# A one-row load moved to the head of the load queue of a fused decode kernel

## The chip, the cores and the metric

One core of a Trainium2 chip. The metric is the device time of one execution in microseconds (us). Most executions agree within a few tenths of a us. All runs here are of the fast state. Ratios are the mean time of one kernel's fast runs over the mean of the other's fast runs of the same rounds; they are not quite the ratio of the medians that are also quoted. The profiled span is about 1.3 us shorter than the device time (194.8 against 196.06 us in the profiled run of the kernel before).

## The reference

```python
W = min(4096, max(256, Sk // 4))                  # 4096 of 16384 cached positions
q = (x @ wq).reshape(B, Sq, Hq, Dh)               # B 4, Sq 1, Hq 32, Dh 128, D 512
k, v = k_cache[:, :, Sk - W:, :], v_cache[:, :, Sk - W:, :]     # 8 kv heads, each for 4 query heads
a = softmax(q @ k.T * Dh ** -0.5) @ v  ->  reshape @ wo
b = ((x @ W_gate) * (x @ W_gate > 0) * (x @ W_up)) @ W_down     # F 1792
g = sigmoid((x * gate_w).sum(-1, keepdims=True))
return g * a + (1 - g) * b
```

(Condensed; not literal code.) Inputs are bf16. The caches and weights that must be read come to 81 MB. `x` is 4 rows of 1 KB, and `gate_w`, the load that the change moves, is one row of 1 KB.

## The kernel before: the parts that matter

All loads are issued by the sync engine on one queue, in the order that `_dma_order` gives. The big ones go to four slots in turn; a load waits until its slot's last reader is done.

```python
def _dma_order():
    o = [("wq",), ("x",), ("gw",), ("k", 0), ("k", 1), ("v", 0)]
    for s in range(2, NSET):
        o += [("k", s), ("v", s - 1)]
    return o + [("wg",), ("wu",), ("v", NSET - 1), ("wd",)] + [("wo", p) for p in range(len(WO_PIECES))]
# ... in sync():
            if k == "x":
                load(("X",), "d_x", xsb[0:4, :], A_x.rearrange("b o d -> (b o) d"))
            elif k == "gw":
                load(("GW",), "d_gw", xsb[4:5, :], gate_w.rearrange("(o p) -> o p", o=1))
            elif k == "wq":
                load(("WQ",), "d_wq", slot("wq"), A_wq.rearrange("(p t) f -> p (t f)", t=4), waits=w)
# ... in tensor(): x and the gate row are transposed together, as five rows
        def XT():
            bk = bankb[tr(("XT",))]
            for q in range(4):
                tp(bk[:, 6 * q:6 * q + 5], xsb[0:5, q:q + 509:4], identb[0:5, 0:5], ev=("XT",) if q == 3 else None,
                   waits=tr_free(("XT",)) + [("X",), ("GW",), ("IDB",)])
# ... order of the program (cut): what TensorE does first and last
    o = [("CONST", k) for k in ("mask", "grp", "rfold")] + [("XT",), ("Z",), ("Q",), ("QT",), ("KT", 0, 0), ...
    o += [("SC", s, 3), ("SW", s), ("PV", s - 1), ("PT", s), ("RS", 1), ("GU",), ("PV", s), ("FFN",), ("OQ",)]
    return o + [("WO", p) for p in range(len(WO_PIECES))]
```

`PV` is the context product of one set of heads and needs its values; `OQ` folds the context; `WO` is the output product, whose weights are the last loads.

## Time and profile before

| | kernel before |
|---|---|
| median device time | 196.1 us (3 runs before the prediction, 196.01 to 196.16) |
| loads | 81.01 MB, mean 416 GB/s over the span |
| DVE busy / PE busy | 64% / 62% |

The sync engine's timeline of the kernel before: start us, duration us, what was issued.

```profile
0.80 0.40 SPq L256 DMA_DIRECT2D slots<-in_A_wq_dram  x1
1.26 0.35 SPq L256 DMA_DIRECT2D xsb<-in_A_x_dram  x1
1.66 0.22 SPq L256 DMA_DIRECT2D xsb<-in_gate_w_dram  x1
1.92 1.26 SPq L256 DMA_DIRECT2D slots<-in_A_k_cache_dram  x2
...
49.21 0.54 SPq L256 DMA_DIRECT2D slots<-in_A_k_cache_dram  x1
```

These durations are those of the issue, not of the transfer. The transfers are in the trace's packet records: the first 32 KB packet of the query weights starts at 1.81 us.

The timeline of TensorE at the end of the kernel before (in brackets the idle time before the group and what ended it):

```profile
178.49 5.03 PE L320 MATMUL bank<-slots,pT 128*64 128x512 bf16 x32 [5.70 <-DMA slots<-in_A_v_cache_dram]
183.45 1.69 PE L320 MATMUL bank<-slots,hg 128*4 128x256 bf16 x28
185.07 1.93 PE L320 MATMUL bank<-osb,fold 128*64 128x256 bf16 x16
188.07 2.02 PE L320 MATMUL bank<-slots,oq 128*4 128x256 bf16 x34 [1.06 <-DMA slots<-in_A_wo_dram]
190.83 1.15 PE L320 MATMUL bank<-slots,oq 128*4 128x256 bf16 x18 [0.73 <-DMA slots<-in_A_wo_dram]
192.20 0.82 PE L320 MATMUL bank<-slots,oq 128*4 128x256 bf16 x12 [0.23 <-DMA slots<-in_A_wo_dram]
```

TensorE waits for output weights three times: the loads set the end, and TensorE keeps up.

### The profile page before, as it was taken

The numbers are of one execution on the slowest core, as the hardware profiler recorded it, in microseconds if no ns is written. First come the engines' busy times: TensorE is split into PE (matmuls) and PEld (weight loads), VectorE is DVE, ScalarE is ACT, GpSimd is POOL, SyncE is SP. The second block draws the span as 40 slices with busy tenths as digits, with TensorE's granted clock in tenths as the row PEclk, the third lists the DMA queues.
The fourth block names the chain that finished last, engine by engine and source line by source line (L and its number), as shares of the span: only waits on it lengthen the run. The fifth ranks groups of instructions, "written<-read, shape, count | busy, mean of one in ns | idle before, by whom it ended". The sixth has DMA issues, their size and how long they took to land.

```text
span 194.8 us, 1734 instructions
## 1 busy us (share of the span) xinstructions
PE 120.6 (62%) x723; PEld 50.6 (26%) x723; DVE 124.1 (64%) x153; ACT 27.5 (14%) x34; POOL 9.5 (5%) x25
## 2 busy tenths in 40 slices
PE   0209279474943894686468943894586466743974
PEld 0003123121411341242112411341142122311562
DVE  6103769999399809980998199819981998370010
ACT  2213000040130013001300130013001300420100
POOL 7830000000000000000000000000000000000000
PEclk9999958999999797899876999697999889997899
DMA  6999999999999999999999999999999999999992
GB/s 215 431 432 431 437 437 431 431 427 451 431 437 437 446 427 424 431 437 431 431 431 431 427 424 437 444 437 431 431 431 421 431 395 427 470 431 384 425 404 90
DMA packets 3616, 81.10 MB, mean 416 GB/s; under 512 B 401, under 2 KB 666, under 8 KB 794
## 3 DMA queue, kind: packets, MB, share of 16 engines
q1 hardware_dynamic: 3610, 81.01, 97.3%
q8 instruction: 5, 0.08, 0.2%
q14 instruction: 1, 0.01, 0.0%
HBM read 81.01 MB, written 0.00 MB: 416 GB/s over the span
## 4 chain that ended last, share of the span: by engine, by line
DMA 54%; DVE 31%; PE 9%; issue 4%; SPq 0%; ACT 0%
DMA slots<-in_A_k_cache_dram 38%; DVE kt L491 21%; DMA slots<-in_A_wo_dram 10%; PE bank L320 7%; DMA xsb<-in_A_x_dram 6%; DVE sc L527 5%; DVE qblk L517 1%; PE bank L324 1%; DVE pT L542 1%; DVE rd L531 1%; SPq L256 0%; DVE negmax L537 0%; ACT gwB L600 0%; DVE osum L577 0%; DVE mx L527 0%
## 5 line engine op out<-in xcount | busy, mean ns | idle before, releaser
L491 DVE STREAM_TRANSPOSE kt<-slots 128x2048 f32<-128x2048 f32 x32 | 73.7, 2305 | 28.1 <-DMA slots<-in_A_k_cache_dram 28.0
L320 PE MATMUL bank<-kt,qblk 128*128 128x512 bf16 x256 | 72.1, 434 | 27.9 <-DVE kt L491 27.9
L320 PEld LDWEIGHTS bank<-kt,qblk 128*128 128x128 bf16 x256 | 25.2, 107 | 69.7 <-DVE kt L491 36.0
L320 PE MATMUL bank<-slots,pT 128*64 128x512 bf16 x256 | 32.3, 410 | 5.7 <-DMA slots<-in_A_v_cache_dram 5.7
L619 ACT ACTIVATE pe<-sc,negmax 128x2048 bf16<-128x2048 bf16 x8 | 16.0, 2002 | 60.1 <-DVE negmax L537 60.1
L527 DVE CUSTOM_DVE_ANT_0 sc<-bank,maskf 128x512 bf16<-128x512 f32 x32 | 21.0, 658 | 3.8 <-PE bank L320 3.7
L320 PEld LDWEIGHTS bank<-slots,pT 128*64 128x64 bf16 x256 | 15.1, 118 | 23.2 <-issue 13.4
L542 DVE STREAM_TRANSPOSE pT<-pe 128x2048 bf16<-128x2048 bf16 x8 | 18.5, 2312 | 2.2 <-ACT pe L619 2.2
L604 ACT ACTIVATE osb<-bank 128x512 bf16<-128x512 f32 x8 | 4.8, 597 | 81.5 <-PE bank L320 81.5
L320 PE MATMUL bank<-rd,grpb 128*128 128x32 bf16 x8 | 1.6, 194 | 22.1 <-DVE rd L531 22.1
L555 DVE TENSOR_TENSOR oq<-bank,recip 64x128 bf16<-64x128 f32 x2 | 0.9, 434 | 12.3 <-PE bank L320 12.2
L320 PEld LDWEIGHTS bank<-rd,grpb 128*128 128x128 bf16 x8 | 0.8, 98 | 25.7 <-DVE rd L531 25.7
L495 DVE COPY xT<-bank 128x20 bf16<-128x20 bf16 x1 | 0.2, 171 | 8.0 <-PE bank L324 8.0
L320 PE MATMUL bank<-slots,oq 128*4 128x256 bf16 x64 | 4.0, 272 | 2.0 <-DMA slots<-in_A_wo_dram 2.0
L320 PE MATMUL bank<-slots,xT 128*4 128x512 bf16 (+1 forms) x64 | 5.0, 467 | 0.0
L320 PE MATMUL bank<-maskr,maskl 128*128 128x512 bf16 x1 | 0.6, 609 | 5.9 <-POOL maskr L296 5.9
L517 DVE TENSOR_SCALAR qblk<-bank 32x64 uint32<-32x64 uint32 x16 | 2.9, 215 | 2.1 <-PE bank L324 2.1
L324 PE MATMUL bank<-identb,xsb 5*128 5x5 bf16 x4 | 0.3, 168 | 5.7 <-DMA xsb<-in_A_x_dram 5.7
L577 DVE CAST osum<-bank 4x256 bf16<-4x256 f32 x1 | 0.4, 418 | 5.2 <-PE bank L320 5.2
L320 PEld LDWEIGHTS bank<-slots,oq 128*4 128x4 bf16 x64 | 2.5, 84 | 3.5 <-DMA slots<-in_A_wo_dram 2.9
L296 POOL TENSOR_SCALAR_AFFINE_SELECT fold<-fold 128x256 bf16<-128x256 bf16 x8 | 3.3, 417 | 1.1
L486 DVE MEMSET qblk<- 128x2304 uint32 x1 | 2.0, 1978 | 1.3 <-PEq L644 1.3
(59 smaller groups left out, 40.3 us busy)
## 6 DMA issues: line engine op xcount, KB each, us to landing
slots<-in_A_k_cache_dram SPq DMA_DIRECT2D x8, 4096.0 KB, 25.1
slots<-in_A_v_cache_dram SPq DMA_DIRECT2D x8, 4096.0 KB, 30.5
slots<-in_A_wq_dram SPq DMA_DIRECT2D x1, 4096.0 KB, 12.4
slots<-in_A_wo_dram SPq DMA_DIRECT2D x1, 2176.0 KB, 17.1
slots<-in_B_W_gate_dram SPq DMA_DIRECT2D x1, 1792.0 KB, 19.7
slots<-in_B_W_up_dram SPq DMA_DIRECT2D x1, 1792.0 KB, 23.6
slots<-in_B_W_down_dram SPq DMA_DIRECT2D x1, 1792.0 KB, 18.5
slots<-in_A_wo_dram SPq DMA_DIRECT2D x1, 1152.0 KB, 19.5
```

Source lines behind the costliest of these rows:

```text
L296: op(lambda: e.affine_select(dst, src, pattern, cmp, fill, base=base, channel_multiplier=mult), ev)
L320: E.op(lambda: t.matmul(out_, lhsT, rhs, start=start, stop=stop, tile_position=pos, skip_group_check=True), ev=ev, waits=waits)
L324: E.op(lambda: t.transpose(out_, in_, idn), ev=ev, waits=waits)
L486: E.op(lambda: v.memset(qblk[:, :, :, :, :].rearrange("p s h c e -> p (s h c e)"), 0.0), ev=("QZ",))
L491: E.op(lambda: v.transpose(kt[:, f, :].bitcast(FP32), slot("k", s)[:, 4096 * f:4096 * f + 4096].bitcast(FP32)), ev=("E", "KT", s, f), waits=w)
L517: E.op(lambda dst=dst, r=r, g=g: v.tensor_scalar(dst, src[r, g, 0:B, :, :], 0, None, op0=ALU.bitwise_or), ev=("E",) + keys[1] if (q, g) == ...
L527: E.op(lambda: v.tensor_tensor_reduce(sc[:, 512 * f:512 * f + 512], banks[scb(key)], R["maskf"][:, :], 1.0, -3.0e38, ALU.add, ALU.max, mx4 ...
L531: E.op(lambda: v.tensor_tensor(rd32[:, :, :], bc(R["own8"][:, :].unsqueeze(2), 2, 4), bc(mx4[:, :].unsqueeze(1), 1, 8), ALU.mult), ev=("MA ...
L542: E.op(lambda: v.transpose(pT[:, s % 2, :], pe[:, :]), ev=("E", "PT", s), waits=[("EXP", s)] + ([("PV", s - 2)] if s >= 2 else []))
L555: E.op(lambda g=g, r=r: v.tensor_tensor(oq[r, :, :].rearrange("p i b -> p b i"), banks[tr(key)][0:64, 128 * g:128 * g + 128].rearrange("p ...
L604: E.op(lambda: a.activation(osb[:, s, :], ob(s), ACTF.Copy), ev=("NORM", s), waits=[("PV", s)])
L619: E.op(lambda: a.activation(pe[:, :], sc[:, :], ACTF.Exp, bias=negmax[:, s % 2:s % 2 + 1], scale=SCALE, accum_out=rowsum[:, s:s + 1]), ev= ...
```

## The change

The gate row's load is issued first of all, the query weights second and x third. The intent is to have the small load out of the way before the large ones fill the queue.

```diff
 def _dma_order():
-    o = [("wq",), ("x",), ("gw",), ("k", 0), ("k", 1), ("v", 0)]
+    o = [("gw",), ("wq",), ("x",), ("k", 0), ("k", 1), ("v", 0)]
```

Nothing else differs.

## The prediction

> What bounds the kernel now: one stream of loads. The DMA part of the profile shows 81.01 MB at a mean of 416 GB/s over the 194.8 us span; in the 40 slices DMA is busy 9 tenths or more in all but the first (6, 215 GB/s) and the last (2, 90 GB/s), at about 431 GB/s. No compute engine comes near: DVE is busy 64%, PE 62%. The packet records show 16 engines each moving a 32 KB row in 1.21 us, back to back from 2 to about 192 us. The issues on the sync engine show that the queue never runs dry: a key load lands 25.1 us after its issue in the median and takes 9.7 us of the stream. So time = start of the stream + bytes / rate + a tail (last landing 192.6; the last 12 matmuls, a cast of 0.42, the store, about 1.2 us).
>
> The chain of waits names other things (38% key loads, 31% DVE, 6% load of x), because it follows one consumer; its early part has slack behind the stream.
>
> What the change does. It removes, adds and resizes nothing. Before, the sync engine issues the query weights (4 MB) at 0.80, x (4 rows) at 1.26, the gate row (1 KB) at 1.66 and the first keys at 1.92 us. The gate row costs 0.27 us from start to start (0.22 busy). After: query weights near 1.06, x near 1.53, first keys still near 1.92.
>
> Gain: nearly none. The transposes of x and the gate row wait for both loads, and x still stands behind the 4 MB. The Trainium skill (DMA: Bandwidth & Descriptors, section Queues, rings and completion order) says each engine consumes its ring in order; the trace agrees: x lands at 13.14 and the gate row at 13.05, both with the last of the query weights (13.15). The same page (section Why a DMA increments its semaphore by 16 and not by 1) says that a one-row load runs on one engine; the gate row's semaphore has two updates only, which fits. Its packet leaves the stream of one engine (tens of ns) and lands near 3 us, of no use before x.
>
> Cost: the stream begins later by the gate row's issue, 0.27 us, all on the critical path, if the first packet still follows the issue of the query weights by 1.0 us (0.80 to 1.81 before). It may be less: the first packets are slow (1.9 to 2.3 us instead of 1.21), and if the gate row takes over part of a cold start, the shift shrinks towards 0. The front of compute (13.1 to 23 us) shifts as much, off the path.
>
> Predicted: 196.3 us, 195.9 to 196.7 eight times in ten. Chances: faster by over 2% 0.01, within 2% 0.98, slower 0.01.
>
> What would show it. Query weights issued near 1.06 us. First 32 KB packet at 2.0 to 2.1 us instead of 1.81. Gate row landing near 3 us; the x transposes still start at 13.2 to 13.5, released by x. The last landing of the output weights moves from 192.6 by as much as the first packet; the tail is unchanged, and so are the slices.
>
> What would make it wrong. A cold start that the tiny load absorbs: the time stays or falls by 0.1 to 0.3. A one-row first load that holds up issue for longer. A different balance between the 16 engines, whose last landings spread over some 2 us, so that another ends last.

## More of the kernel before

The page of the kernel before, three parts. The strings have one digit for each of 40 slices of the span; a 9 means 90% busy or more, PEclk is TensorE's granted clock in tenths.

```profile
span 194.8 us, 1734 instructions
PE 120.6 (62%) x723; PEld 50.6 (26%) x723; DVE 124.1 (64%) x153; ACT 27.5 (14%) x34; POOL 9.5 (5%) x25
...
PEclk9999958999999797899876999697999889997899
DMA  6999999999999999999999999999999999999992
GB/s 215 431 432 431 437 437 431 431 427 451 431 437 437 446 427 424 431 437 431 431 431 431 427 424 437 444 437 431 431 431 421 431 395 427 470 431 384 425 404 90
...
q8 instruction: 5, 0.08, 0.2%
```

The loads hardly pause between the first slice and the last. So the time is the moment at which this stream starts, plus its length, plus what remains after the last landing.

## The result

| | before | after |
|---|---|---|
| median, first comparison (6 runs each) | 196.08 us (195.98 to 196.16) | 196.5 us (196.4 to 196.82) |
| ratio | | 1.0026, 95% interval 1.0013 to 1.0038 |
| issue of the query weights, start to end | 0.80 to 1.20 | 1.18 to 1.54 |
| first 32 KB packet | 1.81 | 2.15 |
| gate row landed | 13.05 | 2.06 |
| x landed | 13.14 | 13.25 |
| last landing of output weights | 192.60 | 192.87 |
| issue of the store of the result | 193.54 | 193.93 |

The lower rows are of one profiled run of each kernel; packets are from the packet records, landings from the semaphore updates of the trace. The change costs about a quarter of a per cent.

The same parts of the page of the kernel after:

```profile
span 195.2 us, 1734 instructions
PE 122.2 (63%) x723; PEld 51.6 (26%) x723; DVE 124.3 (64%) x153; ACT 27.5 (14%) x34; POOL 9.5 (5%) x25
...
PEclk9999958999799699999789987699969799996699
DMA  6999999999999999999999999999999999998992
GB/s 215 430 431 430 430 430 430 430 426 443 430 430 430 445 436 433 430 436 430 436 430 430 433 436 443 430 436 430 430 436 426 423 387 426 477 430 382 430 398 78
```

The stream is as dense as before, within the digits. The sync engine's timeline after:

```profile
0.80 0.32 SPq L256 DMA_DIRECT2D xsb<-in_gate_w_dram  x1
1.18 0.37 SPq L256 DMA_DIRECT2D slots<-in_A_wq_dram  x1
1.59 0.32 SPq L256 DMA_DIRECT2D xsb<-in_A_x_dram  x1
1.95 1.25 SPq L256 DMA_DIRECT2D slots<-in_A_k_cache_dram  x2
```

The query weights start 0.38 us later, which is more than the 0.27 us that the gate row's place took when it stood third. The first keys are issued at nearly the same moment as before (1.95 instead of 1.92). Since the keys have to queue behind the query weights anyway, that does not help.

The end of TensorE's timeline after:

```profile
178.86 6.34 PE L320 MATMUL bank<-slots,pT 128*64 128x512 bf16 x32 [5.75 <-DMA slots<-in_A_v_cache_dram]
185.13 1.69 PE L320 MATMUL bank<-slots,hg 128*4 128x256 bf16 x28
186.76 1.94 PE L320 MATMUL bank<-osb,fold 128*64 128x256 bf16 x16
189.76 3.66 PE L320 MATMUL bank<-slots,oq 128*4 128x256 bf16 x64 [1.07 <-DVE oq L555]
```

In this execution the last context product took 6.34 us instead of 5.03. A stretch at half the TensorE clock, 6.8 us long, began at 177.5 us (the two sixes near the end of PEclk; the exact times are in the trace's clock records); in the profile before it was 3.4 us long from 177.9 us. All 64 output matmuls then ran without a wait, so here TensorE ended last. From the last landing to the store's issue took 1.06 us (193.93 − 192.87) instead of 0.94 (193.54 − 192.60). The chain of waits (the profile's path back from the last instruction, at each step to what released it) shows the same: before, it ended in the output weights' landing; after, it goes through TensorE.

```profile
171.74 20.41 DMA slots<-in_A_wo_dram
192.16 0.04 issue
192.20 0.87 PE bank L320 x12
```

That was the chain before; this is the chain after:

```profile
178.86 9.85 PE bank L320 x76
...
189.76 3.70 PE bank L320 x64
```

Is this second difference part of the change, or luck of one execution? That, and where the rest comes from, is what the experiments are for.

### The profile page after: what moved, and what is told of

It reads as the page before. It is cut to its first block, busy times and chain, and to the rows that moved or that the text cites. A ratio compares the mean times of both kernels' runs of the same rounds, so it can differ in the third digit from the quotient of the medians.

```text
span 195.2 us, 1734 instructions
## 1 busy us (share of the span) xinstructions
PE 122.2 (63%) x723; PEld 51.6 (26%) x723; DVE 124.3 (64%) x153; ACT 27.5 (14%) x34; POOL 9.5 (5%) x25
## 4 chain that ended last, share of the span: by engine, by line
DMA 40%; DVE 25%; PE 22%; issue 9%; POOL 2%; ACT 1%; POOLq 0%
DMA slots<-in_A_k_cache_dram 25%; PE bank L320 20%; DVE kt L491 18%; DMA slots<-in_A_v_cache_dram 15%; DVE sc L527 4%; PE bank L324 2%; DVE qblk L517 1%; POOL maskr L296 1%; DVE oq L555 0%; DVE rd L531 0%; DVE negmax L537 0%; ACT gwB L600 0%; ACT maskf L597 0%; POOL maskl L296 0%; POOL e L296 0%
## 5 line engine op out<-in xcount | busy, mean ns | idle before, releaser
L320 PE MATMUL bank<-slots,pT 128*64 128x512 bf16 x256 | 33.0, 416 | 5.8 <-DMA slots<-in_A_v_cache_dram 5.8
```

The source lines that it names most:

```text
L320: E.op(lambda: t.matmul(out_, lhsT, rhs, start=start, stop=stop, tile_position=pos, skip_group_check=True), ev=ev, waits=waits)
```

## The experiments

The theories:

- **A**: the whole stream starts later, because the gate row's issue holds the sync engine before the query weights. The cost is that issue and nothing else.
- **B**: the loss is in the tail, through half clock on TensorE there (**B2**: the end is the later of the loads and TensorE's last work, which makes the slow runs).
- **C**: a cold start of the DMA engines delays the first packets, and a small load ahead takes part of it over.
- **F**: run-to-run luck of which DMA engine has to fetch instructions.

All kernels gave correct results. Each run is compared with runs of the kernel before from the same rounds on the same chip: the first group stood on chip 0; e_gw_late and the three e_v7 on chip 6; e_gw_half and the three e_oq on chip 12. The edits are cut to the lines that matter. They are shown against the kernel before, except e_gw5 (against the changed kernel) and e_oq (against e_v7).

### First group: what stands ahead of the query weights

The kernel before in these rounds: median 196.15 us (195.92 to 196.39, 9 runs).

**e_after**: the changed kernel again, unedited.

> The changed kernel again, as the anchor of this group. Theory A (the stream of loads starts later because the gate row's issue stands ahead of the query weights): 196.4 to 196.6 us, ratio 1.0015 to 1.003; query weights issued near 1.18 us, first 32 KB packet near 2.15 us. Rival B (the loss sits in the tail: TensorE at half clock while the last context product runs) says the excess over the kernel before changes from run to run, with some runs near 196.1 and some near 196.8.

Measured: 196.53 us (196.19 to 196.81), ratio 1.0019 (1.0007 to 1.0032). Query weights issued at 1.17 us, first 32 KB packet at 2.14. In this profile TensorE waited for output weights again, so the loads ended last although there was a 6.8 us stretch of half clock from 175.7 us:

```profile
178.81 5.48 PE L320 MATMUL bank<-slots,pT 128*64 128x512 bf16 x32 [5.66 <-DMA slots<-in_A_v_cache_dram]
...
192.55 0.82 PE L320 MATMUL bank<-slots,oq 128*4 128x256 bf16 x12 [0.23 <-DMA slots<-in_A_wo_dram]
```

The profiled time was 196.42 us, as slow as the other profile (196.45). So the changed kernel is slower without the tail effect too. As B expected, the runs spread; but the kernel before spread by 0.47 us as well.

**e_gw5**: four more copies of the one-row load, into an unused tile, ahead of the gate row.

```diff
-    o = [("gw",), ("wq",), ("x",), ...
+    o = [("j", 0), ("j", 1), ("j", 2), ("j", 3), ("gw",), ("wq",), ("x",), ...
+                load(("J", it[1]), f"d_j{it[1]}", R["junk"][it[1]:it[1] + 1, :], gate_w.rearrange("(o p) -> o p", o=1))
```

> Four more one-row loads of the gate row into an unused tile stand ahead of everything; five small issues precede the query weights. A: each costs its issue, 0.27 to 0.38 us start to start, so the query weights are issued near 2.3 us instead of 0.80 and the time is before + 1.2 to 1.5, 197.3 to 197.6 us. Rival C (a fixed cold start of the DMA engines is what delays the first packets, and small loads ahead take it over): the first 32 KB packet comes less than 1.0 us after the query weights' issue, and the time is 0.3 to 0.5 us less than A says, below 197.2 us. B: no more than the changed kernel, 196.5 us.

Measured: 197.66 us (197.4 to 197.84), ratio 1.008 (1.0066 to 1.0093), just above A's band. The timeline of the sync engine:

```profile
0.80 1.18 SPq L257 DMA_DIRECT2D junk<-in_gate_w_dram  x4
2.02 0.25 SPq L257 DMA_DIRECT2D xsb<-in_gate_w_dram  x1
2.31 0.37 SPq L257 DMA_DIRECT2D slots<-in_A_wq_dram  x1
```

The first 32 KB packet came at 3.30 us, 0.61 us after the end of that issue, exactly as before the change (1.20 to 1.81). C falls: small loads ahead shorten nothing. B, which allowed 196.5 us, falls as the cause of this loss too.

**e_gw_x_first**: gate row, x, then the query weights.

```diff
-    o = [("wq",), ("x",), ("gw",), ...
+    o = [("gw",), ("x",), ("wq",), ...
```

> Gate row, then x, then the query weights. A: two issues ahead, query weights near 1.55 us, time before + 0.6 to 0.75, 196.7 to 196.9 us. x lands near 3 us and the transposes of x start near 6 us instead of 13.3; the query matmuls then start with the landing of the query weights near 13.5, some 1 us earlier than in the changed kernel, and that gains nothing. A theory that the front of compute is on the path expects a gain of up to 1 us against that.

Measured: 196.86 us (196.61 to 197.13), ratio 1.0037 (1.0024 to 1.0049), as A said; query weights issued at 1.47 us. x had landed at 2.51 us, its transposes ran at 7.39, and the query product waited for its weights alone:

```profile
13.77 3.58 PE L320 MATMUL bank<-slots,xT 128*4 128x512 bf16 x32 [4.84 <-DMA slots<-in_A_wq_dram]
```

That product started 1 us earlier than in the changed kernel (14.80). The kernel became slower all the same: an earlier front bought nothing, a later stream cost its delay.

**e_gw_act**: the gate row first of all, but from the scalar engine's queue.

```diff
-    o = [("wq",), ("x",), ("gw",), ...
+    o = [("wq",), ("x",), ...                 # sync engine
+        E.op(lambda: a.dma_start(xsb[4:5, :], gate_w.rearrange("(o p) -> o p", o=1)), ev=("GW",), ctr="d_gw")   # scalar engine, first
```

> The gate row is still issued first of all, but by the scalar engine's queue; the sync engine starts with the query weights at 0.80 us as in the kernel before, then x. A: the stream starts at 1.81 us again, and the time is that of the kernel before, 195.9 to 196.2 us, ratio 0.999 to 1.0005. If what costs is a gate-row packet or its early landing (not the issue slot on the sync engine), it stays at 196.4 to 196.6.

Measured: 196.23 us (195.91 to 196.48), ratio 1.0004 (0.9991 to 1.0016). The gate row is issued at 0.79 us and does not hold the sync engine:

```profile
0.79 0.50 ACTq L587 DMA_DIRECT2D xsb<-in_gate_w_dram  x1
0.79 0.40 SPq L256 DMA_DIRECT2D slots<-in_A_wq_dram  x1
```

The first 32 KB packet is at 1.81 us again, and the loss is not to be seen. So the early gate row itself costs nothing; its place on the sync engine does. The interval would still allow a small loss.

Put together, the delay of the end of the query weights' issue against the measured change (ratio − 1, times the 196.15 us of before):

| kernel | end of issue | delay | first 32 KB packet | change in time |
|---|---|---|---|---|
| before | 1.20 | 0 | 1.81 | 0 |
| e_gw_act | 1.19 | −0.01 | 1.81 | +0.08 |
| e_after | 1.51 | 0.32 | 2.14 | +0.37 |
| e_gw_x_first | 1.83 | 0.64 | 2.46 | +0.73 |
| e_gw5 | 2.68 | 1.48 | 3.30 | +1.57 |

The time follows the delay one to one, within 0.1 us, where each interval is about 0.25 us wide to either side.

The semaphore records show the same for the stream alone, without what comes after it. A big load lands in 16 parts, each with a semaphore update. I take the mean of the 16 for the last piece of the output weights that has 16, in the profile of each kernel. In the seven profiles of all groups (e_gw_late aside) whose first 32 KB packet comes at 1.81 to 1.84 us, this mean is 191.31 to 191.46, on average 191.40 us. In the four with the changed front it is 191.69 to 191.77, on average 191.72; in e_gw_x_first 191.99, in e_gw5 192.85. So the stream ends 0.32, 0.59 and 1.44 us later for delays of 0.32 to 0.35, 0.64 and 1.48 us.

### How much delay the front of compute can bear

**e_gw_late**: the gate row behind the first keys.

```diff
-    o = [("wq",), ("x",), ("gw",), ("k", 0), ("k", 1), ("v", 0)]
+    o = [("wq",), ("x",), ("k", 0), ("gw",), ("k", 1), ("v", 0)]
```

> Query weights, x, first keys, and only then the gate row. The transposes of x wait for a gate row that stands behind another 4 MB, so they start near 22.9 us instead of 13.2 and the whole front of compute is 9.7 us late. Theory A (only the start of the stream and its length count; the front has slack): 195.9 to 196.4 us, ratio 0.999 to 1.001. A theory that the front of compute sets the time (the chain of waits of the kernel before gave 6% to the load of x) expects up to 9.7 us more.

Measured: 197.05 us (196.73 to 197.9), ratio 1.0055 (1.0038 to 1.0071), against 196.13 us (11 runs of the kernel before in this group). A miss: I had taken the slack of the front to be larger than it is. The page and the timelines tell why. The transposes of x started at 23.03 us, and everything behind moved with them, including the release of the slots:

```profile
GB/s 221 435 436 435 442 455 441 435 435 441 425 428 328 428 428 423 428 431 428 428 428 428 428 428 425 428 428 428 435 448 415 438 412 427 458 441 395 436 394 83
```

```profile
23.03 0.27 PE L324 MATMUL bank<-identb,xsb 5*128 5x5 bf16 x4 [15.51 <-DMA xsb<-in_gate_w_dram]
...
59.87 0.54 SPq L256 DMA_DIRECT2D slots<-in_A_k_cache_dram  x1
```

One slice, near 60 us, fell to 328 GB/s. A key load that the kernel before issues at 49.21 us was issued at 59.87, and adding its issue (0.54) and the 0.61 us from issue to first packet, it could not move data before 61.0 us, while the packet records show the queue running out from 60.5 us. The loads lost about 1 us once and the kernel never got it back (the mean of the last output weights' landings is 192.49 us, 1.04 later than in the kernel before). So a front that is 9.8 us late is already too late.

**e_gw_half**: a delay half as long. The first keys are loaded in two halves with the gate row between them.

```diff
-    o = [("wq",), ("x",), ("gw",), ("k", 0), ("k", 1), ("v", 0)]
+    o = [("wq",), ("x",), ("ka",), ("gw",), ("k", 0), ("k", 1), ("v", 0)]   # ka: columns 0 to 8191 of the first keys
# (cut: ka is loaded into the first keys' slot, ("k", 0) loads the other half, and the reader waits for both)
```

> As e_gw_late, which lost 0.9 us because its front came 9.8 us late and a key load was issued at 59.9 us when the queue had just run dry (in the kernel before: 49.2 us). Here the first keys are loaded in two halves and the gate row stands between them, so the front is about 4.9 us late. A (the front has some 10 us of slack and a delay below it costs nothing): the key load that came at 59.9 comes near 54 to 55 us, DMA stays busy, 195.9 to 196.3 us, ratio 0.999 to 1.001. If a late front costs in proportion, about 0.45 us more than before.

Measured: 196.2 us (196.02 to 196.61), ratio 0.9999 (0.9986 to 1.0012), against 196.3 us for the kernel before (11 runs, 195.88 to 196.6). The transposes started 5.0 us later than before and the key load was issued 5.35 us later (54.56 instead of 49.21):

```profile
18.25 0.27 PE L329 MATMUL bank<-identb,xsb 5*128 5x5 bf16 x4 [10.72 <-DMA xsb<-in_gate_w_dram]
...
54.56 0.54 SPq L256 DMA_DIRECT2D slots<-in_A_k_cache_dram  x1
```

No loss is to be seen. A front that is 5 us late costs nothing measurable, so the few tenths by which the change moves it should not matter. The limit lies between 5 and 9.8 us; where exactly is not measured.

### The tail, and a version that might beat both

**e_v7**, **e_v7_gw**, **e_v7_act**: the last values are loaded ahead of the gate and up weights, with the front of before, of after, and with gate row and x issued by the scalar engine.

```diff
-    return o + [("wg",), ("wu",), ("v", NSET - 1), ("wd",)] + ...
+    return o + [("v", NSET - 1), ("wg",), ("wu",), ("wd",)] + ...
-    ... ("PT", s), ("RS", 1), ("GU",), ("PV", s), ("FFN",), ("OQ",)]
+    ... ("PT", s), ("RS", 1), ("PV", s), ("GU",), ("FFN",), ("OQ",)]
```

> The front of the kernel before; at the end the last values are loaded before the gate and up weights, and TensorE does their product before the gate and up product. The last context product is then over by about 180 us, so a half-clock stretch of TensorE there can no longer hold up the end. Theory B2 (the end is the later of two: the stream's last landing, or the last context product and what follows, which loses about 1.7 us for 3.4 us more at half clock): the fast runs of the kernel before stay (195.9 to 196.1), those above 196.25 go; median 195.9 to 196.1. If the spread has another cause (the instruction fetch that takes one DMA engine for 1.05 us, differing by engine), the spread of about 0.5 us stays as it is.

> The same end with the front of the changed kernel. A: e_v7 + 0.24 to 0.38 us, that is 196.2 to 196.4 us. B2: no run above 196.6, where the changed kernel had 196.8. If the spread is the instruction fetch, runs at 196.7 to 196.8 stay.

> The same end, with gate row and x issued by the scalar engine's queue: the sync engine issues the query weights at 0.80 and the first keys near 1.25 us. A: the stream starts at 1.81 as in the kernel before, so the time is that of e_v7 within 0.1 us: 195.9 to 196.1, faster than both kernels by at most 0.1%. x and the gate row land near 3 us and the query product starts 1 us earlier than before, which gains nothing.

Measured, against the kernel before at 196.13 us (195.95 to 196.35): e_v7 196.23 (195.95 to 196.37), ratio 1.0005 (0.9993 to 1.0017); e_v7_gw 196.76 (196.27 to 197.12), ratio 1.0031 (1.0019 to 1.0043); e_v7_act 196.19 (195.95 to 196.19), ratio 1.0 (0.9988 to 1.0012). A's shift shows again, but larger than its band: the median of e_v7_gw lies 0.53 us above that of e_v7, not 0.24 to 0.38. The runs above 196.25 (e_v7) and 196.6 (e_v7_gw) did not go, so B2's expectation failed. But the test was not clean: in all three e_v7 profiles the fold of the context, left behind the down product, was now TensorE's late work, and in e_v7_gw and e_v7_act TensorE ended last once more. In e_v7_act x landed at 7.92 us, not near 3: from the scalar engine's queue, but issued 0.54 us behind the query weights, it did not get past them at once. Its query product started at 13.14 us instead of 14.68, and again that gained nothing.

**e_oq**, **e_oq_gw**, **e_oq_act**: the mended test, with the fold ahead as well.

```diff
-    ... ("PT", s), ("RS", 1), ("PV", s), ("GU",), ("FFN",), ("OQ",)]
+    ... ("PT", s), ("RS", 1), ("PV", s), ("OQ",), ("GU",), ("FFN",)]
```

> As e_v7, but the fold of the context (16 matmuls, then its copy on VectorE) stands before the gate and up product and not behind the down product, which in e_v7 had become the new late work of TensorE. Now all but the down product is over by about 182 us and TensorE waits for the output weights' landings near 188 us even with 7 us of half clock. B2 (half clock in the tail makes the slow runs): no wait-free block of 64 output matmuls at the end, median 195.9 to 196.1, no run above 196.25. Rival F (which engine the instruction fetch of 1.05 us falls on, and how late that engine started, makes the spread): spread of 0.4 us stays, median 196.1 to 196.2.

> The same end with the changed kernel's front. A with B2: e_oq + 0.24 to 0.38 us, 196.2 to 196.45, no run above 196.6. A with F: same shift of the median, but runs at 196.7 to 196.8 stay.

> The same end, gate row and x issued by the scalar engine's queue. A: as e_oq within 0.1 us, since the query weights are issued at 0.80 us in both.

Measured, against the kernel before at 196.3 us (195.88 to 196.6, 11 runs): e_oq 196.32 (195.96 to 196.53), ratio 1.0 (0.9986 to 1.0014); e_oq_gw 196.71 (196.35 to 197.66), ratio 1.0027 (1.0007 to 1.0047); e_oq_act 196.4 (196.03 to 197.65), ratio 1.0022 (0.9997 to 1.0048), drawn up by two runs of six at 197.44 and 197.65 for which I have no trace. These two and the 197.66 of e_oq_gw have granted clocks of 0.878 to 0.887, among the lowest of all runs; but a run of e_oq with 0.886 took 195.96, so the clock alone is not shown to be the reason. By medians e_oq_gw lies 0.39 us above e_oq, just over A's band, and e_oq_act within 0.1 us of e_oq, as A said. The spread stayed, against B2. The profile of e_oq shows what the new order brought:

```profile
182.94 1.69 PE L320 MATMUL bank<-slots,hg 128*4 128x256 bf16 x28 [2.22 <-DMA slots<-in_B_W_down_dram]
188.04 5.33 PE L320 MATMUL bank<-slots,oq 128*4 128x256 bf16 x64 [3.42 <-DMA slots<-in_A_wo_dram]
```

TensorE was free early, as planned. But in the profiles of all three a half-clock stretch of 3.4 us came at 188.8 to 189.2 us, on top of the output matmuls themselves, which took 5.33 us for the 64 instead of 3.66. From the last landing (192.62) to the store's issue (193.88) then took 1.26 us instead of 0.94. In the profile of e_gw_x_first, where 6.8 us of half clock from 178.5 us met the last context product in the old order, it took 1.35 us. So half clock can cost 0.3 to 0.4 us of tail where it meets the last work, and it met it in the new order too. None of the six beats the kernel before.

## Why the prediction was right, and where it was off

The range held: 196.5 us lies in 195.9 to 196.7, and the class "within 2%" was right. That alone says little, because the range would have held no change at all (196.1) as well; the point forecast, 0.2 us above 196.1, was about half of what was measured (0.51 and 0.37 us). What the runs bear out is the mechanism. Point by point:

- **One stream of loads bounds the kernel.** Right. Four delays of the stream's start (−0.01 to 1.48 us) came out in the time one to one, within 0.1 us.
- **No gain from the early gate row.** Right. It landed at 2.06 us (I had said near 3), but x landed at 13.25 and the transposes started at 13.34. The profile then put their wait down to "issue" and not to x, which I had named, but x's landing 0.09 us before them agrees. e_gw_x_first went further and landed both by 2.51 us: no gain either. The Trainium skill (*DMA: Bandwidth & Descriptors*, section Queues, rings and completion order) says that each DMA engine consumes its descriptors in ring order; the runs agree: x, issued 0.46 us behind the 4 MB, landed with their last part (13.14 and 13.15 us), and landed at 2.51 us when issued ahead of them.
- **The front is off the path.** Right for this change, and bounded by experiment: 5 us late is free, 9.8 us late empties the queue once and costs 1 us.
- **The cost, "the stream begins later by the gate row's issue, 0.27 us".** The mechanism was right and this term too small. 0.27 us was read from the gate row's place as the third issue. As the first issue it took 0.32 us and 0.38 us from start to start. Since the query weights' own issue became shorter (0.37 instead of 0.40), the end of their issue moved by 1.54 − 1.20 = 0.34 us, and the first packet by 0.34 to 0.35. I had let the point forecast lean towards a smaller shift (196.3, 0.2 above 196.1) for a cold start that would absorb part of it; e_gw5 shows none of that.
- **The tail unchanged.** Half right. In one profile of the changed kernel the tail was 0.12 us longer because TensorE ended last; in the other it was as before (0.95 us). The last landing, which was to move as much as the first packet, moved by 0.27 us in the first profile and 0.34 in the second, where the packet moved by 0.34 in both.
- **What I had listed as possible errors.** "A one-row first load that holds up issue for longer" is the one that came true.

What stays open: the two comparisons gave 1.0026 and 1.0019, that is 0.51 and 0.37 us, and the shift of the stream accounts for 0.34. With e_v7_gw against e_v7 and e_oq_gw against e_oq (0.50 and 0.51 us by their means) there are four comparisons of the changed front, on average 0.47 us. The excess, 0.13 us, is at the edge of the noise, and the mean landing of the stream, 0.32 us later, does not contain it: whether it is real, and from what, is not shown.

Nor is the spread of 0.3 to 0.7 us between runs of one kernel settled. B2 alone doesn't make it, since e_oq kept it; half clock on the last matmuls and F remain candidates. In all fourteen profiles the time is the mean landing used above, plus the lag of the last of the 16 parts behind it (1.07 to 1.37 us), plus the tail up to the issue of the store (0.94 to 1.35 us), plus 2.51 to 2.56 us. So between profiles with the same start of the stream lag and tail differ most, by 0.3 to 0.4 us each, and the mean landing by 0.15.

For the lag, F has a close match in the records but no experiment of its own. Six instruction packets fall into the load stream: five of 16 KB, of 1.02 to 1.11 us each in all profiles but one (0.93 to 1.10 in e_gw_late), and one of 8 KB, of 0.3 us. In the kernel before they start at 40.2, 63.3, 73.0, 111.7, 148.2 and 182.1 us. Up to the load landed at 32.56 the last of the 16 parts comes at most 0.34 us after their mean. In the next load, landed at 43.41, the last part lags by 1.35 us, and after each further packet one more part lands over 1 us after the first: 2 at 72.55, 3 at 82.33, 4 at 121.18, 5 at 150.38, 6 at 188.01. All the other profiles but e_gw_late count up to six in the same way. In e_gw_half the first packet came at 45.0 us; there the load that landed at 42.24 still had a lag of 0.26 us, and the next, at 53.14, had 1.35. In e_gw_late, where the queue ran empty near 61 us after one such packet, no part of the load landed at 72.54 was late any more (all 16 within 0.67 us). This fits that each instruction packet puts one DMA engine behind, which stays behind while the queue is full; the records do not name the engine. How much of the spread between runs of one kernel this makes is not shown.

## What to carry to other kernels

When one stream of loads sets the time, the order of the first issues matters for when the first large load is issued: here one, two and five small issues before it on the same engine were paid in full, and a small load behind it was free as long as its reader had slack (5 us were free, 9.8 were not). A small load that is wanted early belongs on another engine's queue, ahead of the large load; here that removed the cost as far as the noise shows (0.9991 to 1.0016). Moving a load ahead pays only if its reader waits for nothing else: here the same transposes waited for x, and x stayed behind 4 MB.

## What the Trainium skill lacked or had wrong

- *DMA: Bandwidth & Descriptors*, section Specifications, gives about 0.6 us as the first-byte latency on the sync and scalar path and doesn't say there from which moment. On the sync engine these runs agree if it is counted from the end of the issue as the profile shows it: 0.61 to 0.63 us from there to the first 32 KB packet in five kernels, and 1.0 us from its start. On the scalar engine's queue the gate row's packet came 0.39 us after the end of its issue and 0.89 us after its start (e_gw_act: 0.79, 1.29, packet at 1.68).
- The same page, section Issuing engines are not separate DMA queues, calls the sequencer's issue time usually small relative to the DMA. At the head of a stream that bounds the kernel it was 0.34 us of the 0.37 to 0.51 us measured. The time of a one-row issue varied with its place, on which I found nothing there: 0.32 us as the first, 0.22 us third, 0.43 us behind the first keys, 0.50 us first on the scalar engine's queue.
- *Runtime: NRT & Kernel Launch*, section Instruction fetch mechanics, says that instructions are refilled in 16 KiB blocks at a cost that is mostly hidden. The blocks are there (five, 0.08 MB on the instruction queue), each a packet of 0.93 to 1.11 us, and in the kernel before the last part of every load lagged the mean by over 1 us since the first of them. The section doesn't mention what they cost a load stream.
